# Twelve more row groups take their residual from a DVE transpose that goes through DRAM

## The chip, the cores and the metric

The kernel runs on one core of one Trainium2 chip. The time is microseconds of device time for one execution; lower is better. Engines are named as in the profile: PE (TensorE), DVE (VectorE), ACT (ScalarE), POOL (GpSimd, which also issues DMAs), SP (SyncE, which here only issues DMAs).

## The reference

x is 8 x 3136 x 256. A filter is applied along the sequence by FFT, then a low-rank mix along the sequence, then a two-layer network along the channels, each with its input added back:

```
y = irfft(rfft(x, axis=1) * (filt_r + 1j*filt_i), n=3136, axis=1)
u = y + (y^T @ U @ V)^T            # rank 32, along the sequence
out = u + relu(u @ w_ch1) @ w_ch2  # 256 -> 1024 -> 256
```

The last line matters here: u is used twice, as the input of the first product and as the residual that is added to the second.

## The kernel before, in words

**Two halves.** For each of the 8 batches an FFT half makes u, channels on partitions and sequence along the free dimension, in a tile `ut` (two buffers). The network half then takes u in 49 groups of 512 rows of the flattened 8 x 3136 rows; a group may straddle two batches.

**The FFT half of one batch** is a set of generators that are resumed one piece at a time:

- `later_x` loads x in four chunks (L128, issued by POOL, tile `x`, four buffers).
- `f1` (16 pieces, four for each chunk) does the first DFT on PE (L250), ACT copies it to `asb` (L255), SP writes it to DRAM (`ct1`, `ct0`, L257, L258).
- `mid` (17 pieces) reads it back turned (L331), does the second DFT on PE (L384), multiplies by the filter on DVE (L392, L396, L397: "the products"), does the first inverse DFT on PE (L345) three products later, has ACT copy it (L355), and SP write it to DRAM (`ct2`, L364, three parts).
- `load_e2` has SP read these rows back (L416), into the tile `eb`, in two halves (h = 0 and 1) for each of the three parts: "the rows".
- `rank` makes the low-rank term on PE and ACT (L423 to L435); DVE spreads it over `eb` in four copies (L438).
- `s4` (16 pieces) does the last inverse DFT on PE (L456) from `eb`; DVE (L463) and ACT (L461) copy it into `ut`. The first eight pieces read half 0 of `eb`, the others half 1.

**The network half** has 8 steps for each group, 392 in all. In each step `mm1` makes one of eight slices of the hidden layer of group n (L488), ACT applies the ReLU (L491, one instruction a step, so its n-th instance dates step n), and `mm2` does an eighth of the second product of group n-1 (L544). Every fourth step finishes two 128-row blocks, which DVE moves from PSUM to `och` (L556); every eighth step POOL writes `och` to DRAM (L561, `out`).

**The residual** comes in two ways. For most groups `residual` adds u on PE: `ut` is loaded as weights and multiplied by an identity, eight matmuls of 128 columns for a group that lies in one batch (L536). For a *turned* group (`turned`, number 37 and up, `FIRST_TURNED`) `turn_u` lets DVE transpose u in 32 x 32 blocks (L515, two instructions for a group), SP writes the result to DRAM in four pieces (L520) so that the blocks change place, and reads it back into `tur` (L524); DVE then adds it when it evicts (L552), and PE does nothing.

**The order** is written out by hand. `plan` has a list for each of the 392 steps; after `mm1` and `mm2` of a step, each generator in its list is resumed once. `deal` spreads a generator's pieces over a range of steps. For batch b, a = S[b-1] and z = S[b] are the first steps of batches b-1 and b in the network half (S is 0, 48, 96, 144, 192, 240, 288, 336, and 392 at the end), and e lies 17, 20 or 22 steps before z. Products of batch b run from about a-5 to e-4, rows around e, the low-rank term from e to e+6, `s4` from e+8 to z-2. The plan only sets the order of instructions on each engine. An engine that issues DMAs runs ahead of the steps until something it needs is missing, and what stands behind a waiting instruction on its queue waits too.

Of the kernel before, what the change touches and what calls it, by code (L numbers as in the profile page):

```python
# [10 lines left out]
F16 = mybir.dt.float16  # L11
# [3 lines left out]
NB = 8  # L15
# [3 lines left out]
DM = 256  # L19
# [1 line left out]
NH = 1024  # L21
GT = 512
NG = NB * SEQ // GT
FIRST_TURNED = 37

# [53 lines left out]
def kernel(  # L81
# [11 lines left out]
    nc = tc.nc  # L93
# [15 lines left out]
    sb = ctx.enter_context(tc.tile_pool(name="sb", bufs=1))  # L109
    ps = ctx.enter_context(tc.tile_pool(name="ps", bufs=2, space=bass.MemoryType.PSUM))  # L110

    def bank(tag, name, dtype=F32):

        return ps.tile([128, 512 if dtype == F32 else 1024], dtype, tag=tag, bufs=4 if tag == "z" else 2, name=name)

    def dram(t, off, dims):
        return bass.AP(tensor=t, offset=off, ap=[list(d) for d in dims])
# [5 lines left out]
    xt = {}  # L123

    def load_x(b, c):
        t = sb.tile([98, 8 * DM], F16, tag="x", bufs=4, name="x")
        for a, n in ((0, 96), (96, 2)) if b == 0 else ((0, 98),):
            nc.gpsimd.dma_start(t[a:a + n], dram(x.tensor, (b * SEQ + 8 * c + 32 * a) * DM, [[32 * DM, n], [1, 8 * DM]]))  # L128
        xt[b, c] = t
# [10 lines left out]
    for c in range(4):  # L140
        load_x(0, c)
# [64 lines left out]
    tu = eb[0:RANK, 0:12, :].rearrange("p r d -> p (r d)")  # L206
# [34 lines left out]
    def f1(b):  # L241
        for c in range(4):
            t = xt[b, c].rearrange("p (j d) -> p j d", d=DM)
            asb = sb.tile([98, 8, DM], F16, tag="asb", bufs=4, name="asb")
            for half in range(2):
                for i in range(2):
                    pf = bank("z", "pf")
                    for s in range(2):
                        j = 4 * half + 2 * i + s
                        nc.tensor.matmul(pf[0:98, 256 * s:256 * s + 256],  # L250
                                         ws[:, (8 * c + j) * 98:(8 * c + j + 1) * 98], t[:, j, :],
                                         start=(s == 0), stop=True, skip_group_check=True)
                    dst = asb[:, 4 * half + 2 * i:4 * half + 2 * i + 2, :]
                    src = pf[0:98].rearrange("p (j d) -> p j d", d=DM)
                    nc.scalar.copy(dst, src)  # L255
                    if half and i:
                        nc.sync.dma_start(dram(ct1[b], 8 * c * 96 * DM, [[DM, 96], [96 * DM, 8], [1, DM]]), asb[0:96])  # L257
                        nc.sync.dma_start(dram(ct0[b], 8 * c * DM, [[32 * DM, 2], [1, 8 * DM]]),  # L258
                                          asb[96:98].rearrange("p j d -> p (j d)"))
                    yield  # L260
# [151 lines left out]
    def load_e2(b, part, hs=(0, 1)):  # L412

        n = 12 if (b, part) == (0, 2) else 16
        for h in hs:
            nc.sync.dma_start(eb[32 + part:32 + 4 * n:4, 32 * h:32 * h + 32, :].rearrange("p (q r) d -> p q (r d)", r=8),  # L416
                              dram(ct2[b][part], 8 * h * DM, [[NR * DM, n], [16 * DM, 4], [1, 8 * DM]]))
# [61 lines left out]
    groups = [Group(n) for n in range(NG)]  # L479

    def utv(b):
        return ut[b].rearrange("p h q r -> p h (q r)")
# [11 lines left out]


    def turned(gr):
        return gr.n >= FIRST_TURNED

    def turn_u(gr):

        t = sb.tile([128, 4, 4, 2, 32], F16, tag="asb", bufs=4, name="tu")
        for dh in range(2):
            for b, t0, o, n in gr.seg:
                j, z = o // 32, (o + n) // 32
                while j < z:

                    k = min(z, j + 4 - j % 4) if j % 4 or z - j < 4 else z - z % 4
                    src = utv(b)[:, dh, t0 + 32 * j - o:t0 + 32 * k - o]
                    if k - j < 4:
                        dst = t[:, j % 4:j % 4 + k - j, j // 4, dh, :]  # L510
                        src = src.rearrange("p (c e) -> p c e", e=32)
                    else:
                        dst = t[:, :, j // 4:k // 4, dh, :].rearrange("p c g e -> p g c e")
                        src = src.rearrange("p (g c e) -> p g c e", c=4, e=32)
                    nc.vector.transpose(dst, src)  # L515
                    j = k
            yield
        td = nc.dram_tensor(f"tu_{gr.n}", (128, 4 * DM), F16, kind="Internal")
        for a in range(4):
            nc.sync.dma_start(dram(td, DM * a, [[4 * DM, 32], [128 * DM, 4], [1, DM]]),  # L520
                              t[32 * a:32 * a + 32].rearrange("i c g h e -> i c (g h e)"))
        yield
        gr.tu = sb.tile([128, 4, 4, 2, 32], F16, tag="x", bufs=4, name="tur")
        nc.sync.dma_start(gr.tu.rearrange("p a g h e -> p (a g h e)"), td.ap())  # L524
        yield

    def residual(gr, o, i):
# [10 lines left out]
    def mm2(gr, t):  # L538
        i, half = t // 2, t % 2
        if t % 4 == 0:  # L540
            gr.pc = bank("o", "pc")
        o = gr.pc[:, 256 * (i % 2):256 * (i % 2) + 256]
        for tt in range(4 * half, 4 * half + 4):
            nc.tensor.matmul(o, gr.h[tt][:, 128 * i:128 * i + 128], w2sb[:, tt, :],  # L544
                             start=(tt == 0), stop=(tt == 7 and turned(gr)), skip_group_check=True)
        if half and not turned(gr):
            residual(gr, o, i)
        if t % 4 == 3:
            if t == 3:
                gr.och = sb.tile([128, 4, DM], F32, tag="och", bufs=2, name="och")  # L550
            if turned(gr):
                nc.vector.tensor_add(gr.och[:, i - 1:i + 1, :].rearrange("p g (h a e) -> p (g h) a e", h=2, a=4),  # L552
                                     gr.pc.rearrange("p (f a e) -> p f a e", f=4, a=4),
                                     gr.tu[:, :, i - 1:i + 1].rearrange("p a g h e -> p (g h) a e"))
            else:
                nc.vector.tensor_copy(gr.och[:, i - 1:i + 1, :], gr.pc.rearrange("p (j d) -> p j d", d=DM))  # L556
            if gr.n == NG - 1:
                nc.sync.dma_start(dram(out.tensor, (gr.n * GT + 128 * (i - 1)) * DM, [[DM, 128], [128 * DM, 2], [1, DM]]),
                                  gr.och[:, i - 1:i + 1, :])
            elif t == 7:  # L560
                nc.gpsimd.dma_start(dram(out.tensor, gr.n * GT * DM, [[DM, 128], [128 * DM, 4], [1, DM]]), gr.och)  # L561
# [3 lines left out]
    plan = [[] for _ in range(8 * NG)]  # L565

    def deal(gen, count, a, z):
        for i in range(count):
            plan[max(0, int(a + i * (z - a) / count))].append(gen)

    def later_x(b, c):
        load_x(b, c)
        yield

    f1s = [f1(b) if b > 1 else f1_turned(b) for b in range(NB)]
    mids = [mid(0, "o")] + [mid(b) for b in range(1, NB)]
    ranks = [rank(b) for b in range(NB)]
    s4s = [s4(b) for b in range(NB)]
    turns = [turn_u(gr) for gr in groups]

    u_hat()
# [4 lines left out]
    for i in range(16):  # L586
# [3 lines left out]
        next(f1s[0])  # L590
    nc.gpsimd.dma_start(sv[32:97], sv_d.rearrange("k (r q) -> k r q", q=NQ))
    load_x(1, 0)
    nc.gpsimd.dma_start(w1sb, moe_w_ch1.rearrange("(h dd) c -> dd h c", h=2))
    spread_filters(2)
# [29 lines left out]
    for _ in s4s[0]:  # L624
        pass

    def loads(b, part):
        load_e2(b, part)
        yield

    for b in range(1, NB):
        a, z = S[b - 1], S[b]
        e = z - (17 if b == 1 else 20 if b < 6 else 22)
        deal(mids[b], 13, a + {1: 8, 2: -3}.get(b, -5), e - 4)
        deal(mids[b], 4, e - 4, e)
        for p, at in enumerate((e - 5, e - 4, e + 1)):
            plan[at].append(loads(b, p))
        deal(ranks[b], 6, e, e + 6)
        deal(s4s[b], 16, e + 8, z - 2)
        if b == 1:  # L640
            deal(f1s[1], 12, 1, 8)
        if b + 1 < NB:
            for c in range(4):
                plan[a + (9 + 2 * c if b == 1 else 1 + 4 * c)].append(later_x(b + 1, c))
            deal(f1s[b + 1], 16, a + (21 if b == 1 else 10), z - (13 if b == 1 else 20))

    for gr in groups:
        if turned(gr):
            for i in range(4):
                plan[8 * gr.n + (0, 1, 2, 5)[i]].append(turns[gr.n])  # L650
    for n, gr in enumerate(groups):
        for t in range(8):
            mm1(gr, t)
# [36 lines left out]
```

## Time and profile before

| | us |
|---|---|
| median of 3 runs | 518.17 (514.89 to 519.52) |
| the profiled execution, its own time | 516.43 |
| its span, first to last instruction | 514.6 |
| PE busy | 490.5 (95%) |
| ACT busy | 377.1 (73%) |
| DVE busy | 366.2 (71%) |
| POOL busy | 80.6 (16%) |

The granted TensorE clock is 0.995 of full speed. A share of the span is an average over stages; what a change is worth is read from the stage in which it lies. In a row of a group of instructions, the first number after the bar is the time in which at least one of them ran, the next the mean length of one in ns; matmuls overlap, so the length of one is not what it adds to the time. In a timeline, each line has the start, the length in us, the engine and the line of the code, and in brackets the idle time of the engine before it with what ended that.

### The profile page before, as it was taken

The numbers are of one execution on the slowest core, as the hardware profiler recorded it, in microseconds if no ns is written. First come the engines' busy times: TensorE is split into PE (matmuls) and PEld (weight loads), VectorE is DVE, ScalarE is ACT, GpSimd is POOL, SyncE is SP. The second block draws the span as 40 slices with busy tenths as digits, with TensorE's granted clock in tenths as the row PEclk, the third lists the DMA queues.
The fourth block names the chain that finished last, engine by engine and source line by source line (L and its number), as shares of the span: only waits on it lengthen the run. The fifth ranks groups of instructions, "written<-read, shape, count | busy, mean of one in ns | idle before, by whom it ended". The sixth has DMA issues, their size and how long they took to land.

```text
span 514.6 us, 11909 instructions
## 1 busy us (share of the span) xinstructions
PE 490.5 (95%) x4754; PEld 349.6 (68%) x4754; DVE 366.2 (71%) x497; ACT 377.1 (73%) x704; POOL 80.6 (16%) x122
## 2 busy tenths in 40 slices
PE   3887899999999999999999999999999998999996
PEld 3645566776767777777767777777677765676665
DVE  5886599579847986679747986679846997853332
ACT  6874778867986689667986689667886676666663
POOL 6662010002001110002001110002001000011110
PEclk9998999999999999999999999999999999999999
DMA  8987926957877286837877286837877136644454
GB/s 187 175 206 174 181 74 172 281 171 176 216 229 251 69 186 190 298 130 177 213 227 254 69 185 202 262 156 184 218 228 240 65 126 206 212 153 149 126 162 163
DMA packets 76016, 94.52 MB, mean 184 GB/s; under 512 B 5795, under 2 KB 58979, under 8 KB 75960
## 3 DMA queue, kind: packets, MB, share of 16 engines
q1 hardware_dynamic: 61256, 52.17, 33.9%
q0 software_dynamic: 14704, 41.58, 31.4%
q8 instruction: 37, 0.61, 0.5%
q14 instruction: 19, 0.16, 0.1%
HBM read 58.35 MB, written 50.92 MB: 212 GB/s over the span
## 4 chain that ended last, share of the span: by engine, by line
PE 81%; DVE 8%; DMA 4%; issue 1%; ACT 1%; SPq 0%; POOL 0%; DVEq 0%; POOLq 0%
PE pc L544 31%; PE phh L488 30%; DVE uv L392 5%; PE pu L456 5%; PE pf L250 4%; PE pe L345 4%; PE pz L384 3%; PE pc L536 3%; DMA w2sb<-in_moe_w_ch_dram 2%; PE ph L423 1%; DVE uv L397 1%; DMA eb<-ct 1%; DVE uv L396 1%; DMA ct<-e 1%; DVE och L556 1%
## 5 line engine op out<-in xcount | busy, mean ns | idle before, releaser
L491 ACT ACTIVATE h<-phh 128x512 f16<-128x512 f32 x392 | 235.9, 603 | 83.2 <-PE phh L488 81.7
L544 PE MATMUL pc<-w2sb,h 128*128 128x256 f16 x1568 | 233.7, 272 | 1.2 <-DMA w2sb<-in_moe_w_ch_dram 1.2
L488 PE MATMUL phh<-ut,w1sb 128*128 128x512 f16 (+7 forms) x896 | 233.3, 352 | 0.4 <-DVE ut L463 0.4
L544 PEld LDWEIGHTS <-h 128*128 128x128 f16 x1568 | 151.7, 97 | 91.8 <-issue 1.5
L392 DVE TENSOR_TENSOR uv<-pz,fab 128x1024 f16<-128x1024 f32 (+1 forms) x104 | 120.6, 1177 | 12.5 <-PE pz L384 10.5
L561 POOL DMA_DIRECT2D out_dram<-och x48 | 39.1, 814 | 402.0 <-DVE och L556 318.8
L488 PEld LDWEIGHTS <-w1sb 128*128 128x128 f16 x896 | 78.9, 97 | 19.8 <-issue 1.5
L556 DVE COPY och<-pc 128x512 f32<-128x512 f32 x74 | 51.0, 689 | 44.4 <-PE pc L536 43.5
L355 ACT CAST e<-pe 128x512 f16<-128x512 f32 x96 | 56.6, 591 | 21.0 <-PE pe L345 20.2
L463 DVE CAST ut<-pu 128x392 f16<-128x392 f32 x92 | 48.5, 557 | 17.9 <-PE pu L456 16.0
L255 ACT CAST asb<-pf 98x512 f16<-98x512 f32 x96 | 57.3, 599 | 0.2
L438 DVE COPY eb<-h 32x4096 f16<-32x4096 f16 x32 | 38.2, 1232 | 14.2 <-ACT h L435 14.2
L552 DVE TENSOR_TENSOR och<-pc,tur 128x512 f32<-128x512 f32 x24 | 16.5, 689 | 39.8 <-PE pc L544 37.3
L345 PE MATMUL pe<-uv,m 128*128 128x512 f16 (+1 forms) x117 | 41.3, 371 | 3.6 <-DVE uv L392 1.5
L456 PE MATMUL pu<-sv,eb 97*128 97x49 f16 x1024 | 40.5, 187 | 3.3 <-DMA eb<-ct 3.1
L456 PEld LDWEIGHTS <-eb 97*128 97x128 f16 x1024 | 37.7, 98 | 4.8 <-DVE eb L438 3.4
L536 PE MATMUL pc<-idn,ut 128*128 128x128 f16 (+1 forms) x302 | 40.8, 219 | 0.0
L384 PE MATMUL pz<-a,m 128*128 128x512 f16 x96 | 36.2, 379 | 1.1 <-DVE a L311 1.0
L250 PE MATMUL pf<-x,ws 98*98 98x256 f16 x192 | 36.6, 273 | 0.0
L396 DVE TENSOR_TENSOR uv<-uv 64x1024 f16<-64x1024 f16 (+1 forms) x49 | 30.9, 630 | 1.7
L536 PEld LDWEIGHTS <-ut 128*128 128x128 f16 (+1 forms) x302 | 28.8, 98 | 3.9 <-issue 0.6
L397 DVE TENSOR_TENSOR uv<-uv 64x1024 f16<-64x1024 f16 (+1 forms) x49 | 30.7, 627 | 0.7
(80 smaller groups left out, 264.9 us busy)
## 6 DMA issues: line engine op xcount, KB each, us to landing
out_dram<-och POOLq DMA_DIRECT2D x48, 512.0 KB, 4.4
ct<-e SPq DMA_DIRECT2D x47, 256.0 KB
eb<-ct SPq DMA_DIRECT2D x46, 256.0 KB
x<-in_x_dram POOLq DMA_DIRECT2D x28, 392.0 KB, 7.8
ct<-asb SPq DMA_DIRECT2D x24, 384.0 KB
a<-ct SPq DMA_DIRECT2D x18, 512.0 KB
tu<-tu SPq DMA_DIRECT2D x48, 64.0 KB
tur<-tu SPq DMA_DIRECT2D x12, 256.0 KB
```

Of the source, the lines that this page charges most:

```text
L250: nc.tensor.matmul(pf[0:98, 256 * s:256 * s + 256], ws[:, (8 * c + j) * 98:(8 * c + j + 1) * 98], t[:, j, :], start=(s == 0), stop=True, s ...
L255: nc.scalar.copy(dst, src)
L345: nc.tensor.matmul(pe[:, 0:n], w, uv[:, f, o:o + n], start=(f == 0), stop=(b > 0 or f == 1))
L355: nc.scalar.copy(t[:, 2 * (i % 2):2 * (i % 2) + 2, :].rearrange("p k d -> p (k d)"), pe)
L384: nc.tensor.matmul(pz, a2m, src[:, k:k + 2, :].rearrange("p k d -> p (k d)"), start=True, stop=True)
L392: nc.vector.tensor_mul(uv[:, :, o:o + n], zin, fin)
L456: nc.tensor.matmul(pu[:, NQ * i:NQ * i + NQ], eb[:, 8 * n + i, d], sv[:, 8 * g + i, :], start=(i == 0), stop=True, skip_group_check=True)
L488: nc.tensor.matmul(ph[:, o:o + n], w1sb[:, dh, 128 * t:128 * t + 128], utv(b)[:, dh, t0:t0 + n], start=(dh == 0), stop=(dh == 1), skip_gro ...
L491: nc.scalar.activation(h, ph, RELU)
L536: nc.tensor.matmul(d, w, idn, start=False, stop=(dh == 1), skip_group_check=True)
L544: nc.tensor.matmul(o, gr.h[tt][:, 128 * i:128 * i + 128], w2sb[:, tt, :], start=(tt == 0), stop=(tt == 7 and turned(gr)), skip_group_check ...
L556: nc.vector.tensor_copy(gr.och[:, i - 1:i + 1, :], gr.pc.rearrange("p (j d) -> p j d", d=DM))
```

## The change

For batches 1 to 6 (b in the loop over the plan), the last two groups before the border step z, numbers z/8-2 and z/8-1, are turned as well: 4, 5, 10, 11, 16, 17, 22, 23, 28, 29, 34 and 35. `turn_at` holds the four steps at which each group's generator is resumed. For the first of the two the DVE transposes are at e-3 and e-2, for the second at e-1 and e; the writes to DRAM are at z-14 and z-13, the reads at z-10 and z-8. These DMAs are issued by POOL; those of the old turned groups stay with SP. `FIRST_TURNED` becomes 38, so group 37 has its residual on PE again. So 23 groups are turned instead of 12.

The new tiles have tags of their own, `tu` and `tur`, two buffers each; `x` and `asb` have three buffers instead of four, and three of the first x chunks use buffers of `asb`. The fourth x chunk of a batch is loaded two steps later (a+15, not a+13), for batch 2 ten steps later (25, not 15).

The rows of batches 1 to 7 are read half by half: half 0 of the three parts where both halves were (e-5, e-4, e+1), half 1 of all three at e+2.

```
-FIRST_TURNED = 37
+FIRST_TURNED = 38
     def load_x(b, c):
-        t = sb.tile([98, 8 * DM], F16, tag="x", bufs=4, name="x")
+        tag = "asb" if (b, c) in ((0, 3), (1, 0), (1, 1)) else "x"
+        t = sb.tile([98, 8 * DM], F16, tag=tag, bufs=3, name="x")
...
     def turned(gr):
-        return gr.n >= FIRST_TURNED
+        return gr.n >= FIRST_TURNED or gr.n in turn_at
     def turn_u(gr):
-        t = sb.tile([128, 4, 4, 2, 32], F16, tag="asb", bufs=4, name="tu")
+        t = sb.tile([128, 4, 4, 2, 32], F16, tag="tu", bufs=2, name="tu")
...
+        queue = nc.sync if gr.n >= FIRST_TURNED else nc.gpsimd
         for a in range(4):
-            nc.sync.dma_start(dram(td, DM * a, [[4 * DM, 32], [128 * DM, 4], [1, DM]]),
+            queue.dma_start(dram(td, DM * a, [[4 * DM, 32], [128 * DM, 4], [1, DM]]),
...
-        gr.tu = sb.tile([128, 4, 4, 2, 32], F16, tag="x", bufs=4, name="tur")
-        nc.sync.dma_start(gr.tu.rearrange("p a g h e -> p (a g h e)"), td.ap())
+        gr.tu = sb.tile([128, 4, 4, 2, 32], F16, tag="tur", bufs=2, name="tur")
+        queue.dma_start(gr.tu.rearrange("p a g h e -> p (a g h e)"), td.ap())
...
-    def loads(b, part):
-        load_e2(b, part)
+    def loads(b, parts, h):
+        for part in parts:
+            load_e2(b, part, [h])
         yield
+    turn_at = {n: [8 * n + i for i in (0, 1, 2, 5)] for n in range(FIRST_TURNED, NG)}
...
-        for p, at in enumerate((e - 5, e - 4, e + 1)):
-            plan[at].append(loads(b, p))
+        for at, parts, h in ((e - 5, [0], 0), (e - 4, [1], 0), (e + 1, [2], 0), (e + 2, range(3), 1)):
+            plan[at].append(loads(b, parts, h))
+        if b < NB - 1:
+            turn_at[z // 8 - 2] = [e - 3, e - 2, z - 14, z - 10]
+            turn_at[z // 8 - 1] = [e - 1, e, z - 13, z - 8]
...
-                plan[a + (9 + 2 * c if b == 1 else 1 + 4 * c)].append(later_x(b + 1, c))
+                plan[a + (9 + 2 * c + 10 * (c > 2) if b == 1 else 1 + 4 * c + 2 * (c > 2))].append(later_x(b + 1, c))
...
-    for gr in groups:
-        if turned(gr):
-            for i in range(4):
-                plan[8 * gr.n + (0, 1, 2, 5)[i]].append(turns[gr.n])
+    for n, at in turn_at.items():
+        for i in at:
+            plan[i].append(turns[n])
```

## The prediction, made before the changed kernel was run

> **What bounds the kernel now.** I read the page first, then the waits of PE, then the timeline of single steps, and last DVE's timeline where it feeds PE.
>
> ```profile
> PE 490.5 (95%) x4754; PEld 349.6 (68%) x4754; DVE 366.2 (71%) x497; ACT 377.1 (73%) x704; POOL 80.6 (16%) x122
> ...
> L536 PE MATMUL pc<-idn,ut 128*128 128x128 f16 (+1 forms) x302 | 40.8, 219 | 0.0
> ```
>
> PE is busy nearly all the time, and the residual (L536) has 302 matmuls in it. Whether PE sets the time everywhere is told by its waits, asked for 62 to 430 us, which is the network half with batches 1 to 7 beside it:
>
> ```profile
> PE pz L384 <- DVE a L311: 1.0, 2, 0.7
> ```
>
> This is the whole answer: 1.0 us in 368. So between 62 and 430 us every PE instruction lengthens the run by what it takes on PE. What a residual matmul takes is read from PE's timeline of bare steps:
>
> ```profile
> 152.32 0.59 PE L488 MATMUL phh<-ut,w1sb 128*128 128x512 f16 x2
> 152.75 0.60 PE L544 MATMUL pc<-w2sb,h 128*128 128x256 f16 x4
> 153.19 0.59 PE L488 MATMUL phh<-ut,w1sb 128*128 128x512 f16 x2
> 153.62 0.60 PE L544 MATMUL pc<-w2sb,h 128*128 128x256 f16 x4
> 154.06 0.28 PE L536 MATMUL pc<-idn,ut 128*128 128x128 f16 x2
> 154.17 0.59 PE L488 MATMUL phh<-ut,w1sb 128*128 128x512 f16 x2
> ```
>
> From L488 to L488 is 0.87 us without residual and 0.98 with two of its matmuls: 0.055 us each. By the page's row it would be 40.8/302 = 0.135, but that row counts overlapped time, so I take 0.055.
>
> After 430 us PE waits once for the products of batch 7:
>
> ```profile
> 432.12 0.39 PE L345 MATMUL pe<-uv,m 128*128 128x512 f16 x1 [1.33 <-DVE uv L397]
> ```
>
> Before it DVE runs without a gap from 401.1 us, and the chain that ended last goes through DVE from 410.6 to 432.1, with group 37's transposes in it:
>
> ```profile
> 416.50 0.71 DVE tu L515
> 417.21 1.11 DVE uv L392
> 418.32 0.62 DVE tu L515
> ```
>
> **Part 1, the residual of twelve groups leaves PE.** Each lies in one batch: 8 matmuls x 0.055 = 0.44 us, twelve times 5.28 us. Group 37 gives 0.44 back, so 88 matmuls net, 4.84 us. By 0.135 it would be 11.9 us, the upper bound of this term.
>
> **Part 2, group 37's transposes leave DVE.** In DVE's timeline they displace 0.64 and 0.61 us (start to next start), 1.25 together, in a stretch that ends in PE's wait. This has to be summed with part 1, since DVE and not PE sets the time there. DVE becomes saturated around step 284 (399.6 us). By then PE is ahead by the ten groups of batches 1 to 5 (4.4 us) and half of group 34 (0.2). From there DVE's string ends 1.25 us earlier: 4.6 + 1.25 = 5.9 us ahead when it releases PE. PE by itself would be 5.28 - 0.44 + 1.33 = 6.2 ahead, so it still waits some 0.3 us and **5.9 us** is the gain at 432 us. Behind that the plan is the old one, so 5.9 reaches the end. Turned evictions cost the same: L552 and L556 both take 689 ns.
>
> **Part 3, the new transposes on DVE.** Four for each of six batches, 0.69 us each (L515, 688 ns): 2.75 us a batch. They stand where DVE has nothing to do, between the last product and the low-rank copies:
>
> ```profile
> 260.32 0.69 DVE L556 COPY och<-pc 128x512 f32<-128x512 f32 x1
> 265.39 0.69 DVE L556 COPY och<-pc 128x512 f32<-128x512 f32 x1 [4.38 <-PE pc L536]
> 268.72 1.22 DVE L438 COPY eb<-h 32x4096 f16<-32x4096 f16 x1 [2.64 <-ACT h L435]
> ```
>
> Two fill 1.4 of the 4.38 us, two 1.4 of the 2.64. In batch 6 the gap is 5.33 us, in batch 1 3.67 and 1.91. I cost them at nothing; without that cover it would be 6 x 2.75 = 16.5 us of DVE time, most of it late for the low-rank copies and so for `s4`.
>
> **Part 4, the trip through DRAM on POOL's queue.** This is what the trace does not show: these DMAs from SP are there, from POOL not. Take the batch whose border is z = 192. On POOL's queue stand `out` (issued at 271.15), eight writes, the first read, the next `out`, the second read. An issue took POOL 0.54 to 0.57 us for an x chunk and 0.75 to 0.80 for `out`, so the writes are out by about 277. The `out` ahead of them landed at 277.64; four writes of 64 KB behind it should land by 279.3. Then the read is issued; a DMA from POOL of twice its size (`out`) lands at best after 3.1 us, so I put it at 282.3. It is needed by the eviction at z-5, which DVE began at 283.76: 1.5 us in hand. The same for the other borders, with `out` landing at 163.22, 219.51, 336.53, 396.24: +0.5, +2, +0.6 and -0.5 us in hand. Border 48 has its writes at step 34 and its need at 43, some 10 us.
>
> If it is late by L, DVE stands still by L, with the last `ut` copies and the products of the next batch behind it. What that costs PE is told by the room between DVE's end of a product and PE's L345 that takes it. The first product of each batch has least: 1.26 us at batch 5, 0.92 to 1.27 elsewhere. PE now comes 0.5 us sooner, so some 0.7 us of lateness is free, and beyond that PE loses L - 0.7 in each batch. Best case L below 0.7 everywhere, no cost. Worst by the rows: a POOL transfer's longest landing is 9.0 us, against the 3.1 that I used, so L = 4 to 5 and some 6 x 4 = 24 us. My estimates lie near the low end; I take 0.3 us in all.
>
> **Where the Trainium skill speaks against this.** One `out` in each batch stands beside the low-rank copies of DVE and is longer:
>
> ```profile
> 155.36 1.13 POOL L561 DMA_DIRECT2D out_dram<-och  x1 [9.07 <-DVE och L556]
> ```
>
> 1.13 us, against 0.75 to 0.80 elsewhere. The Trainium skill, "SBUF — State Buffer", section "Who interferes with whom", says that GpSimd and a VectorE copy in a two-port mode exclude each other for whole instructions, so that descriptors of a GpSimd DMA wait for it. The trace agrees for the issue, 0.35 us longer. By that rule the writes could not begin before the low-rank copies end, and the sum would be about 0.5 us higher at z = 96, where they end at 158.6.
>
> **Part 5, three x buffers, and the fourth chunk later.** The chunk now stands behind the `out` of step a+15 on POOL's queue, where it stood in front. An x chunk just behind an `out` lands 6.0 to 6.3 us after its issue. Issued 0.8 us after that `out`, it lands at 142.0, 199.6, 259.1, 315.4 and 373.7 us for batches 3 to 7, and PE takes it (L250) at 144.2, 201.9, 260.0, 317.7 and 376.2: 0.9 to 2.5 us in hand. For batch 2 it is 93.5 against 95.1, but there the `out` itself landed only at 93.05, and x cannot be before it. Best case nothing. Worst by the rows: the second chunk in a row lands after 8 to 9 us, which would cost 0 to 1.5 us a batch, 3 us in all. I take 0.3 us, for batch 2.
>
> **Part 6, rows by halves.** PE does not wait for rows in 62 to 430 us, so nothing is gained; half 1 is issued at e+2 (about 271 us at z = 192) and needed at 280.9, so nothing is lost. SP's queue has four row reads in a row where it had two, so the reads of the next batch's DFT (L331) start 1.2 us later, at 273 instead of 271.8; they are needed from 283.3.
>
> **Sum:** 5.9 - 0.3 - 0.3 = 5.3 us. The profiled execution took 516.43 (span 514.6), so 511.1 by it. The median of the runs is 1.7 us higher, which would give 512.9. Three runs that spread over 4.6 us do not tell which is typical; I take the middle, **512.0 us**.
>
> **Rivals.**
>
> *The read from DRAM is late and stalls DVE at z-5.* For it: four of five borders have less than 2 us in hand, and DMA is 0.8 to 0.9 busy there. Against: after 282 us DMA is idle until 291. Its place is the eviction at z-5, its price 6 x (L - 0.7): it eats the whole gain at L = 1.7 us and makes the kernel slower by 1% from L = 2.5. With L = 3, 6 x 2.3 = 13.8, so about 520 to 522 us. Chance 0.16.
>
> *The fourth x chunk is late and PE waits at L250.* For it: the 0.9 us at batch 5. Against: that `out` no longer shares the DMA engines with the chunk that stood in front. Worst 3 us: 514.5. With part of both rivals the gain is 1 to 5 us. Chance 0.30.
>
> *DVE takes over as the bound once PE is faster.* PE gains 0.9 us from z-8 to z+8, just where DVE is 98% busy (286 to 294 us). Against: the smallest room is 1.24. If that were all used in each batch, half of part 1 would go, 2.6 us: 514.6. Chance 0.08.
>
> *The forecast* as it stands, 509.5 to 513.5, has 0.46.
>
> **Chances.** Faster by over 1% (a gain of over 5.2 us) 0.42: most of the forecast's case. Within 1% 0.42: its rest and the second and third rivals. Slower by over 1% 0.16. About 1% is what this kernel's runs can tell from no change. The range is 508.0, for a gain that misses the costs and runs as low as the lowest ones shown, to 519.0, which takes in the x chunks, a DVE bound and an L of up to 2.
>
> **What the profile after would show.** L536 with 214 matmuls; steps at z-8 to z-1 of 0.87 us, where nothing else stands in them; L515 without idle time behind it at e; no wait of PE on DVE at batch borders; the wait at 432 us down to about 0.3. Wrong if L552 waits for DMA `tur` by more than 0.7 us at z-5, if L252 on PE (the old L250) waits for DMA x, or if POOL's second `out` after e is held up far enough to keep `och` from DVE.

## The result, and the profile after

The changed kernel takes 521.8 us (median of 6 runs, 521.27 to 528.0); in the same comparison the kernel before takes 515.04. The ratio is **1.0137, 95% interval 1.010 to 1.0174**: slower by 1.4%, where 1% faster was forecast. The profiled execution took 521.29 us (span 519.5), against 516.43 (514.6) before. The ratios here and below leave out runs over 1.5% slower than the fastest of the same kernel, but for the one kernel where the text gives all four times.

The page of the changed kernel, and from its groups by line the residual on PE:

```profile
PE 488.0 (94%) x4666; PEld 343.9 (66%) x4666; DVE 378.0 (73%) x519; ACT 376.7 (73%) x704; POOL 121.5 (23%) x182
```

```profile
L540 PE MATMUL pc<-idn,ut 128*128 128x128 f16 (+1 forms) x214 | 28.7, 220 | 0.0
```

The 88 matmuls are gone (302 before, 214 now). But the span grew while PE's busy time fell. PE's waits in 62 to 445 us say where (columns: who waits at which line for whom, us in total, times, longest). Before, the same list had 1.3 us for batch 7 (L345), the 1.0 us at L384 and 0.2 us at L456:

```profile
PE pu L458 <- DVE ut L465: 4.2, 3, 1.7
PE pz L386 <- DVE uv L394: 3.1, 4, 0.8
PE pz L386 <- DVE a L313: 1.0, 2, 0.7
PE pe L347 <- DVE uv L399: 0.8, 1, 0.8
PE pf L252 <- DMA x<-in_x_dram: 0.3, 1, 0.3
```

PE now waits for DVE in `s4` (L458) and at the first products of the next batch (L386). DVE's timeline at the border z = 192 shows what DVE itself waits for:

```profile
288.08 0.69 DVE L556 TENSOR_TENSOR och<-pc,tur 128x512 f32<-128x512 f32 x1 [3.53 <-DMA tur<-tu]
288.68 0.55 DVE L465 CAST ut<-pu 128x392 f16<-128x392 f32 x1
289.16 1.21 DVE L394 TENSOR_TENSOR uv<-pz,fab 128x1024 f16<-128x1024 f32 x1
```

The first eviction of the first turned group stands 3.53 us for its read from DRAM, with the last `ut` copies and the first product queued behind it. Before, the eviction at this place had 0.62 us of idle time ahead of it, waiting for PE:

```profile
283.76 0.69 DVE L556 COPY och<-pc 128x512 f32<-128x512 f32 x1 [0.62 <-PE pc L536]
```

The first ReLU of each group of eight steps, dated in both traces, gives the loss by border. From eight steps before a border to eight steps after it, the difference after minus before moves by +0.2, +3.5, +3.6, +1.1 and -0.6 us at z = 96, 144, 192, 240 and 288, and PE should have gained 0.88 in each (16 matmuls). So the cost is 1.1, 4.4, 4.4, 1.9 and 0.3 us, **12.1 us in all** against a gain of 5.3. Batch 7 gains another 0.5 us (steps 304 to 323). By step 16 the changed kernel is already 1.6 us ahead; the traces of the twelve kernels with the new plan, which is the same up to there, lie between 2.0 us ahead and 0.6 behind at this step, so this is not put down to the change. Together that makes 4.7 us more, and the span has 4.9. At z = 48 there is no cost: the difference falls by 0.83 us from step 40 to 56, as the matmuls that are gone would have it.

POOL's timeline at z = 192 shows the trip link by link:

```profile
272.68 1.13 POOL L565 DMA_DIRECT2D out_dram<-och  x1 [9.06 <-DVE och L560]
273.80 5.00 POOL L524 DMA_DIRECT2D tu<-tu  x7
281.70 0.55 POOL L524 DMA_DIRECT2D tu<-tu  x1 [2.91 <-DMA out_dram<-och]
284.95 0.56 POOL L528 DMA_DIRECT2D tur<-tu  x1 [2.70 <-DMA tu<-tu]
285.50 0.76 POOL L565 DMA_DIRECT2D out_dram<-och  x1
286.55 0.55 POOL L528 DMA_DIRECT2D tur<-tu  x1 [0.29 <-issue]
```

`out` landed at 281.42, 8.7 us after its issue. The eighth write was not issued before that; the fourth write landed at 284.37, and only then could the read go, which landed at 287.95. The transposes had been finished since 263.9 and 268.8 us:

```profile
262.56 1.30 DVE L517 STREAM_TRANSPOSE tu<-ut 128x512 f16<-128x512 f16 x2
266.91 0.69 DVE L560 COPY och<-pc 128x512 f32<-128x512 f32 x1 [3.04 <-PE pc L540]
267.52 1.29 DVE L517 STREAM_TRANSPOSE tu<-ut 128x512 f16<-128x512 f16 x2
270.25 1.22 DVE L440 COPY eb<-h 32x4096 f16<-32x4096 f16 x1 [1.43 <-ACT h L437]
```

They fill idle time of DVE, as forecast (4.38 became 3.04, and 2.64 became 1.43). Their result lay ready for 5 to 10 us before POOL, waiting to issue `out`, came to it.

### The profile page after: what moved, and what is told of

Read it like the earlier page. It is cut to its first block, busy times and chain, and to the rows that moved or that the text cites. A ratio compares the mean times of both kernels' runs of the same rounds, so it can differ in the third digit from the quotient of the medians.

```text
span 519.5 us, 11773 instructions
## 1 busy us (share of the span) xinstructions
PE 488.0 (94%) x4666; PEld 343.9 (66%) x4666; DVE 378.0 (73%) x519; ACT 376.7 (73%) x704; POOL 121.5 (23%) x182
## 4 chain that ended last, share of the span: by engine, by line
PE 59%; DMA 14%; DVE 10%; issue 7%; POOL 4%; ACT 1%; SPq 0%; DVEq 0%; POOLq 0%
PE pc L548 23%; PE phh L490 22%; DMA tu<-tu 7%; DVE uv L394 5%; PE pf L252 4%; DMA tur<-tu 3%; PE pe L347 3%; DMA x<-in_x_dram 3%; PE pz L386 3%; POOL tu L524 2%; PE pu L458 2%; PE pc L540 1%; POOL out_dram L565 1%; DVE och L556 1%; DVE och L560 1%
## 5 line engine op out<-in xcount | busy, mean ns | idle before, releaser
L556 DVE TENSOR_TENSOR och<-pc,tur 128x512 f32<-128x512 f32 x46 | 31.7, 690 | 55.4 <-PE pc L548 38.6
L560 DVE COPY och<-pc 128x512 f32<-128x512 f32 x52 | 35.7, 687 | 28.8 <-PE pc L540 28.1
L458 PE MATMUL pu<-sv,eb 97*128 97x49 f16 x1024 | 39.2, 185 | 6.8 <-DVE ut L465 4.2
L347 PE MATMUL pe<-uv,m 128*128 128x512 f16 (+1 forms) x117 | 41.3, 371 | 3.1 <-DVE uv L394 1.6
L458 PEld LDWEIGHTS <-eb 97*128 97x128 f16 x1024 | 37.3, 96 | 9.2 <-issue 7.2
L386 PE MATMUL pz<-a,m 128*128 128x512 f16 x96 | 36.7, 384 | 4.2 <-DVE uv L394 3.1
L524 POOL DMA_DIRECT2D tu<-tu x48 | 33.9, 714 | 10.6 <-DMA out_dram<-och 10.6
L517 DVE STREAM_TRANSPOSE tu<-ut 128x512 f16<-128x512 f16 (+2 forms) x50 | 30.2, 643 | 0.2
## 6 DMA issues: line engine op xcount, KB each, us to landing
out_dram<-och POOLq DMA_DIRECT2D x48, 512.0 KB, 3.8
a<-ct SPq DMA_DIRECT2D x18, 512.0 KB
```

Source lines behind the costliest of these rows:

```text
L347: nc.tensor.matmul(pe[:, 0:n], w, uv[:, f, o:o + n], start=(f == 0), stop=(b > 0 or f == 1))
L386: nc.tensor.matmul(pz, a2m, src[:, k:k + 2, :].rearrange("p k d -> p (k d)"), start=True, stop=True)
L458: nc.tensor.matmul(pu[:, NQ * i:NQ * i + NQ], eb[:, 8 * n + i, d], sv[:, 8 * g + i, :], start=(i == 0), stop=True, skip_group_check=True)
L524: queue.dma_start(dram(td, DM * a, [[4 * DM, 32], [128 * DM, 4], [1, DM]]), t[32 * a:32 * a + 32].rearrange("i c g h e -> i c (g h e)"))
```

## The experiments

Each ratio is against the kernel before, on the same chip.

**One group in place of two.** Two theories were set against each other. Theory A: the first read lands after its eviction wants it. Theory B: the trips load POOL and the DMA engines and cost wherever they stand.

```
-            turn_at[z // 8 - 2] = [e - 3, e - 2, z - 14, z - 10]
             turn_at[z // 8 - 1] = [e - 1, e, z - 13, z - 8]
```

> Only the second of the two groups before each border is turned (5, 11, 17, 23, 29, 35); the first has its residual on PE again, everything else is as in the changed kernel. Theory A (the first read from DRAM lands after the eviction at z-5 wants it, and DVE, then PE, stand still): the second read is wanted eight steps later, so DVE does not wait for tur, and the kernel is faster than before by 6 x 0.44 of PE and most of group 37's 1.25 us of DVE, 2.5 to 3.5 us. Rival B (the trips load POOL and the DMA engines, and that costs wherever they stand): half of the loss stays, 3 us slower than before.

512.87 against 516.24 us: 0.9934 (0.9908 to 0.996), 3.4 us faster. DVE does not wait for `tur` in 62 to 445 us, and the idle time ahead of the eviction at z-5 is 0.62 us again. As theory A has it.

**No group before a border.**

```
-        if b < NB - 1:
-            turn_at[z // 8 - 2] = [e - 3, e - 2, z - 14, z - 10]
-            turn_at[z // 8 - 1] = [e - 1, e, z - 13, z - 8]
```

> No group before a border is turned; group 37 has its residual on PE, x and asb have three buffers, the fourth x chunk is later and the rows are read by halves, as in the changed kernel. Theory A: about 1.2 us faster than before (group 37's transposes leave DVE's string), since none of these parts costs anything. Rival C (the fourth x chunk or the rows by halves carry the loss): 2 us or more slower than before, with PE waiting for x at L252 or for rows at L458.

514.36 against 516.24: 0.9971 (0.9945 to 0.9996), 1.5 us faster. Between 62 and 445 us PE waits only for the 1.0 us at L386 (two waits) that it had before at L384. The buffers, the late chunk and the rows by halves carry none of the loss.

**Reads that wait for nothing.** The same number of bytes, the same transposes and writes; but the reads no longer wait for the writes, and go out ahead of them (at z = 192 some 10 us).

```
+        if gr.n < FIRST_TURNED:
+            gr.tu = sb.tile([128, 4, 4, 2, 32], F16, tag="tur", bufs=2, name="tur")
+            nc.gpsimd.dma_start(gr.tu.rearrange("p a g h e -> p (a g h e)"), dram(ct2[0][0], 0, [[4 * DM, 128], [1, 4 * DM]]))
         t = sb.tile([128, 4, 4, 2, 32], F16, tag="tu", bufs=2, name="tu")
...
+        if gr.n < FIRST_TURNED:
+            return
         gr.tu = sb.tile([128, 4, 4, 2, 32], F16, tag="tur", bufs=2, name="tur")
```

> As the changed kernel, but the 12 reads of POOL take as many bytes of rows that have lain in DRAM since batch 0, and stand ahead of the transposes in the order, so that they wait for nothing; the transposes and the 48 writes are as they were. The residual of these 12 groups is therefore not theirs. Theory A: no wait for tur, so the gain that was forecast appears, 5 to 6 us against before. Rival B: the writes and POOL's work are all there, so it stays slower than before by 3 us or more.

511.11 against 516.24: 0.9893 (0.9865 to 0.9922), **5.5 us faster**. So the transposes, the writes and POOL's extra issues cost next to nothing, and the forecast gain is there once the read is in time. Theory B falls.

**The trip on SP's queue.**

```
-        queue = nc.sync if gr.n >= FIRST_TURNED else nc.gpsimd
+        queue = nc.sync
```

> As the changed kernel, but SP issues the writes and reads of the 12 groups, behind the rows and ahead of the reads of the next batch's DFT. Theory A with POOL's queue as what makes the read late (the out of step z-17 ahead of the writes): the read is in tur before z-5, DVE does not wait, and the DFT's reads, some 6 us later than before, cost PE 0 to 2 us a batch: between 5 us faster and 3 us slower than before. If the load of the DMA engines made it late, whoever issues: DVE waits at z-5 for 2 us or more as in the changed kernel.

523.67 against 516.24: 1.014 (1.0111 to 1.0169). `tur` is in time at z = 96 to 288 (0.51 us idle ahead of the eviction, 1.38 at 288), at z = 48 it is 3.1 us late. The cost has moved, as SP's timeline at z = 192 and PE's waits show:

```profile
277.09 6.36 SPq L524 DMA_DIRECT2D tu<-tu  x8
283.62 1.55 SPq L528 DMA_DIRECT2D tur<-tu  x2
285.22 0.43 SPq L333 DMA_DIRECT2D a<-ct  x1
```

```profile
PE pz L386 <- DMA a<-ct: 8.1, 6, 2.7
```

Eight writes and the two reads that wait for them stand ahead of the DFT's reads, 1.6 MB a batch, which now go out after 285 and not at 277, when the writes begin; PE waits for them at L386. Its trace also has three stretches of 3.41 us with a granted clock of 0.50 (from 114.0, 230.1 and 349.6 us; see the last section). The trip was early enough, what stood behind it was not. The direction was left open by theory A; the 0 to 2 us a batch for the DFT's reads was too low.

**What makes POOL's trip late.** Three suspects were taken away: DVE's low-rank copies, which run while POOL issues `out` and the first writes; the DFT's reads, which share the DMA engines; the rows' second halves, which the change put just ahead. A fourth run takes the first two away together, a fifth halves the writes. The first, thinner low-rank copies:

```
+            m = 16 if b in (0, 7) else 1
-            nc.vector.tensor_copy(eb[0:32, 16 * g:16 * g + 16, :],
+            nc.vector.tensor_copy(eb[0:32, 16 * g:16 * g + m, :],
...
```

> As the changed kernel, but in batches 1 to 6 the four low-rank copies of DVE (L440) write one sixteenth of their columns, so that DVE is free while POOL issues the out of step z-17 and the writes. The low-rank term of these batches is therefore missing in most of u. Theory D (the copies hold up POOL's descriptors): out at the borders 144 to 288 lands 4 to 5 us after its issue in place of 5.2 to 9.2, the first read 3 us or more sooner, DVE waits for tur under 1 us a batch, and the kernel is 3 to 6 us faster than before. Theory E (the reads of the next batch's DFT on SP's queue take the DMA engines): the landings and the wait stay, 4 us or more slower than before.

Fewer reads for the DFT:

```
+            if g in (1, 2) and b < 7:
+                a2[g] = a2[0]
+                return
```

> As the changed kernel, but in batches 2 to 6 two of the three 512 KB reads for the DFT (L333) are left out and the first tile is used three times, so that 1 MB less is read just when POOL's out and writes are under way. Two thirds of the frequencies of these batches are therefore wrong. Theory E: out and the writes land 3 us or more sooner, DVE waits for tur under 1 us a batch at the borders 96 to 240 (batch 7 is unchanged), 2 to 6 us faster than before. Theory D: the first packets still come only when the copies end, out lands about 2 us sooner at most, the read is late by 1 us or more, and the kernel is not faster than before by more than 2 us.

Both edits together:

> Thin low-rank copies and fewer DFT reads together (the low-rank term and two thirds of the frequencies of batches 1 or 2 to 6 are therefore not right). If the two together make POOL's transfers late: out at the borders 96 to 240 lands 4 to 5 us after its issue, the idle time ahead of the first eviction at these borders is the 0.6 us of before, and the kernel is 4 us or more faster than before. If the order on POOL's queue makes it (out, eight writes, the read): the idle time stays over 1 us at two or more of these four borders and the gain is under 3 us.

Only the first of the two groups, with half the writes:

```
-            turn_at[z // 8 - 1] = [e - 1, e, z - 13, z - 8]
```

> Only the first of the two groups before each border is turned (4, 10, 16, 22, 28, 34), with its DMAs where the changed kernel has them: four writes between out and the read in place of eight. If the number of writes makes the read late: the read lands 1 to 2 us sooner, DVE waits under 2 us for it, and the time is within 2 us of before. If it is the out ahead of them and the traffic of SP: DVE waits about 3 us at borders 144 and 192 as in the changed kernel, TensorE's clock falls to half behind it, and it is 4 us or more slower than before.

The rows read whole, as before the change:

```
-        for at, parts, h in ((e - 5, [0], 0), (e - 4, [1], 0), (e + 1, [2], 0), (e + 2, range(3), 1)):
-            plan[at].append(loads(b, parts, h))
+        for p, at in enumerate((e - 5, e - 4, e + 1)):
+            plan[at].append(loads(b, p))
...
```

> As the changed kernel, but the rows are read as before, both halves of a part at once, so that 512 KB of them no longer stand just ahead of out and the writes. If these rows make the trip late: out and the writes land 1 to 2 us sooner at borders 144 to 288, the idle time ahead of the first eviction falls from 2.5 to 3.5 to under 2 us, the half clock is gone, and the kernel is within 2 us of before. If they don't: it stays 4 us or more slower than before.

Measured, with the idle time of DVE ahead of the first eviction (0.51 to 0.62 when nothing is late, 1.4 to 1.5 at z = 288):

| | ratio (95%) | z = 96 | 144 | 192 | 240 | 288 |
|---|---|---|---|---|---|---|
| changed kernel | 1.0137 (1.010 to 1.0174) | 1.8 | 3.5 | 3.5 | 2.7 | 2.5 |
| thin copies | 1.0002 (0.9967 to 1.0036) | 1.4 | 1.4 | 1.5 | 2.8 | 2.5 |
| fewer DFT reads | 0.9961 (0.9923 to 0.9999) | 0.9 | 1.6 | 0.5 | 1.6 | 3.2 |
| both | 0.9941 (0.9908 to 0.9974) | 0.6 | 0.9 | 4.8 | 1.6 | 2.8 |
| first group only | 1.0263 (1.020 to 1.0326) | 1.6 | 5.6 | 2.7 | 2.0 | 3.2 |
| rows whole | 1.0126 (1.0068 to 1.0185) | 2.3 | 3.2 | 3.0 | 2.5 | 2.9 |

Each row of idle times is one execution; the one of "both" was the slowest of its ten (516.72 us, the others 509.7 to 515.4), so its borders need not be typical. The ratio of the first group only counts all four runs, 524.3, 525.4, 533.0 and 533.9 us; the two lower ones alone are 1.7% slower than before.

Neither theory holds alone. Without the copies, POOL's timeline at z = 192 has

```profile
270.26 0.78 POOL L566 DMA_DIRECT2D out_dram<-och  x1 [9.05 <-DVE eb L441]
271.03 3.83 POOL L525 DMA_DIRECT2D tu<-tu  x7
277.95 0.55 POOL L525 DMA_DIRECT2D tu<-tu  x1 [3.09 <-DMA out_dram<-och]
280.63 0.57 POOL L529 DMA_DIRECT2D tur<-tu  x1 [2.12 <-DMA tu<-tu]
```

The issues are shorter (0.78 in place of 1.13, seven writes in 3.83 in place of 5.00), as the rule of the Trainium skill ("SBUF — State Buffer", "Who interferes with whom") has it. But `out` still takes 7.4 us to land (270.26 to 277.67), and at the four borders 144 to 288 it lands after 6.7 to 9.3 us, where 4 to 5 were expected. With fewer DFT reads it still takes 7 to 9 us there, though the last writes land closer behind it. With both gone the first two borders are within 0.4 us of being in time, and one read at z = 192 took 5.7 us to land (278.44 to 284.17) with no reason that the trace shows. Half the writes do not help either: at z = 144 the read was issued 2.2 us after the fourth write had landed, and DVE stood 5.6 us. The rows' halves play no part. So copies and traffic each add a microsecond or two at some of the borders, and how much each of them adds, and what makes `out` land late without either, **stays open**. What is common to all six rows is that the trip begins behind `out`.

**Writes ahead of `out`.** The two parts that write and read are put right behind the two that transpose.

```
-            turn_at[z // 8 - 2] = [e - 3, e - 2, z - 14, z - 10]
-            turn_at[z // 8 - 1] = [e - 1, e, z - 13, z - 8]
+            turn_at[z // 8 - 2] = [e - 3, e - 2, e - 1, e + 2]
+            turn_at[z // 8 - 1] = [e - 1, e, e + 1, e + 4]
```

> As the changed kernel, but the writes of the two groups stand at e-1 and e+1, ahead of the out of step z-17 on POOL's queue, and the reads at e+2 and e+4. Theory A: the first read has landed before z-5, DVE does not wait for tur; the rows, whose transfers are now beside the writes, may be up to 2 us later and have some 2 us of room before L458: 3 to 6 us faster than before. If the rows have no room: PE waits at L458 for eb, up to 2 us a batch, and it is from 0 to 6 us slower than before.

511.97 against 516.05: 0.9917 (0.9892 to 0.9943), 4.3 us faster. DVE is back to 0.51 us ahead of the eviction (1.38 at z = 288). PE waits at L458 three times, 1.2 us at z = 48, 0.6 at 144 and 0.5 at 288.

**The same from border 96 on.** With the first border as in the changed kernel:

```
-            turn_at[z // 8 - 2] = [e - 3, e - 2, e - 1, e + 2]
-            turn_at[z // 8 - 1] = [e - 1, e, e + 1, e + 4]
+            turn_at[z // 8 - 2] = [e - 3, e - 2] + ([z - 14, z - 10] if b == 1 else [e - 1, e + 2])
+            turn_at[z // 8 - 1] = [e - 1, e] + ([z - 13, z - 8] if b == 1 else [e + 1, e + 4])
```

> As the run with the writes ahead of out, but at the first border (48) writes and reads stand where the changed kernel has them, since the run before waited 1.4 us there at L458 and the changed kernel did not. Theory A: DVE waits nowhere for tur, PE loses at most 0.7 us at two borders: 4.5 to 6 us faster than before, 1 to 1.5 us faster than with the writes ahead everywhere. If the 1.4 us were chance: no faster than that run, 3 to 4 us faster than before.

510.24 against 515.92: **0.9904 (0.9878 to 0.9929), 5.0 us faster** than before; this version beats both kernels. Over the run above, a gain of 1 to 1.5 us had been expected; it is 0.7 us by the centres of the two ratios, and their intervals overlap, so it is not shown. PE waits at L458 for 0.2 us at z = 96 and 0.8 at 288. Its POOL timeline at z = 192, and the first eviction:

```profile
257.08 0.79 POOL L565 DMA_DIRECT2D out_dram<-och  x1 [9.42 <-DVE och L560]
258.42 2.21 POOL L524 DMA_DIRECT2D tu<-tu  x4 [0.54 <-DVE tu L517]
263.35 3.02 POOL L524 DMA_DIRECT2D tu<-tu  x4 [2.73 <-DVE tu L517]
266.37 1.51 POOL L528 DMA_DIRECT2D tur<-tu  x1
267.87 1.34 POOL L565 DMA_DIRECT2D out_dram<-och  x1
```

```profile
279.31 0.69 DVE L556 TENSOR_TENSOR och<-pc,tur 128x512 f32<-128x512 f32 x1 [0.51 <-PE pc L548]
```

The writes now wait for nothing but the transposes; the read is issued 12.9 us before its eviction and lands at 273.1, 6.7 us after its issue, where the sum of part 4 had 3.1, and still 6 us early.

## Why the prediction was wrong

**The step that failed is part 4**, in both of its figures.

*The landing.* Part 4 put the first read of z = 192 11.1 us after the issue of `out` (271.15 to 282.3). It was 15.3 (272.68 to 287.95). By link: `out` itself 8.7 in place of 6.5, the four writes 3.0 behind it in place of 1.7, the read's issue 0.6 behind them and its landing 3.0 behind that. The read was sized well, its issue was put at nothing; `out` was taken from the trace of before, where nothing stood behind it, and the writes from a guess. I had taken the lowest row for the links that were not shown and kept the longest one (9.0 us) only for an end of the range that the range then did not reach. I had +0.5, +2, +1.5, +0.6 and -0.5 us in hand. Counted from the 0.51 us (1.38 at z = 288) of the runs with a read in time, the measured lateness was 1.3, 3.0, 3.0, 2.2 and 1.1 us.

*Its price.* "Some 0.7 us of lateness is free, and beyond that PE loses L - 0.7" was read from the room between a product and L347. But PE does not get that far. At z = 144, 192 and 240 it stops at L458, two steps on, because DVE's `ut` copies stand behind the waiting eviction; the rest comes at L386, which is where z = 96 has its only wait. PE's timeline at z = 144, changed kernel:

```profile
225.47 0.60 PE L548 MATMUL pc<-w2sb,h 128*128 128x256 f16 x4
227.72 0.37 PE L458 MATMUL pu<-sv,eb 97*128 97x49 f16 x8 [1.65 <-DVE ut L465]
228.84 0.38 PE L386 MATMUL pz<-a,m 128*128 128x512 f16 x1 [0.76 <-DVE uv L394]
229.06 0.59 PE L490 MATMUL phh<-ut,w1sb 128*128 128x512 f16 x2
229.49 0.93 PE L548 MATMUL pc<-w2sb,h 128*128 128x256 f16 x4
```

The costs 1.1, 4.4, 4.4, 1.9 and 0.3 us stand against latenesses 1.3, 3.0, 3.0, 2.2 and 1.1: nearly all of L at z = 96 and 240, 1.4 us more than L at z = 144 and 192, and 0.8 less at 288. I named the `ut` copies as queued behind the eviction and then did not ask who waits for them. By L - 0.7 the measured latenesses would have cost 7.1 us, so the landing, which part 4 priced at 0.3 us, is the larger error. Of the 5.0 us above that, some 3.4 are a halved clock behind the two longest stalls (see the last section), and only the rest is room that was not there.

The rival had the right mechanism and place, and a price too low: its L = 3 at six borders was to cost 13.8 us; a mean of 2.1 at five cost 12.1. Its time does not follow from its own sum: 512.0 less the 0.3 us already in it, plus 13.8, is 525.5 and not 520 to 522. That the measured 521.8 lies in that stretch is luck.

**What was right.** Part 1: 0.055 us a matmul; the reads that wait for nothing gained 5.5 us, where 5.9 less some waits had been forecast, and z = 48 gained 0.83 of 0.88. Part 2: group 37 off DVE with the other parts is 1.5 us (0.2 to 2.8), forecast 1.25; in the trace of the run without border groups, steps 304 to 323 gain 1.24. In the changed kernel PE's wait for batch 7 is down from 1.33 to

```profile
437.60 0.39 PE L347 MATMUL pe<-uv,m 128*128 128x512 f16 x1 [0.76 <-DVE uv L399]
```

where 0.3 had been forecast; in the run whose reads wait for nothing, where PE is as early as forecast, it is 0.2. Part 3: no cost. Part 5: PE waits 0.3 us for x, at one place, as taken. Part 6: neither gain nor loss, and with the rows whole it is as slow. The low-rank copies do lengthen POOL's issues, by what the Trainium skill ("SBUF — State Buffer", "Who interferes with whom") says; but without them the time only falls to that of before, 1.4% or 7 us, where half a microsecond at one border had been reckoned for them. Part 4 took that row as a remark and not into its sum.

## What to carry to other kernels

A tile that goes out and comes back through DRAM is a chain of DMAs, each of which waits for the one before; size each link by the slow rows of the busiest stretch, and issue the first as soon as the data is there. On an engine that only issues DMAs, look for what stands ahead on its queue: here an `out` that waited for an eviction held back writes whose data had been ready for up to 10 us. Price a late operand by the first thing that stops behind the waiting instruction, of any kind, not by the consumer that one has in mind.

## What was not expected of the hardware

**A stall of PE costs more than its length.** The windows of the changed kernel behind the stall at z = 144 (columns: stretch, busy us of PE, PEld, DVE, ACT and POOL with instructions, granted clock, DMA share, GB/s):

```profile
226.00:229.60 3.60, 1.19 (x14) 0.66 (x12) 3.10 (x5) 0.81 (x2) 0.00 (x0) 1.00 0.30 86
229.60:233.00 3.40, 3.40 (x16) 2.02 (x14) 3.32 (x6) 1.19 (x2) 0.00 (x0) 0.50 0.03 5
233.00:236.00 3.00, 3.00 (x27) 2.43 (x26) 2.29 (x3) 2.13 (x4) 1.87 (x3) 1.00 0.43 175
```

After 3.6 us with PE busy for 1.19, the granted clock is 0.50 for 3.41 us, and then full again: four matmuls of a step take 0.85 us from start to next start and not 0.43. That is 1.7 us on top of the stall, and accounts for the two borders that cost 4.4 us; at the three others, with stalls of 2 us and less, the clock stayed at 1.00. The Trainium skill, "TensorE: Matmul & The Clock Gate", section "Part 1: The HAM clock gate (the "warmup" mystery)", has the half clock and its window of about 3.4 us, and puts it behind an idle window. The trace agrees with the size and length; here it came although PE had worked for a third of the time before. In the trace of before there is no such stretch between the first step (51 us) and 512.8 us, only one just ahead of it at 45.2 to 48.6 us, and it stood in no part of the prediction.

How much idle time it takes can be read from the traces. The stretches lie on a grid: 229.61 and 291.05 us, where two of them begin, are 18 windows of 3.413 us apart. From 60 to 445 us, in the traces of before and of all twelve kernels with the new plan, PE was busy for 11 to 51% of the window ahead in the ten cases where a half clock followed, and for 52% or more in all other windows. The changed kernel has 33% at z = 144, 29% at 192 and 57% at 240. As far as these traces go, PE's busy share of such a window decides, with an edge near half, and not one long gap: the longest at z = 144 is 1.65 us.

**A ninth DMA of POOL waits for the first.** In the changed kernel and in the run with thin copies, the eighth write is issued only when the `out` eight DMAs ahead of it has landed (281.42 and 281.70; 277.67 and 277.95). Whether that is the chip's limit or that of the program's semaphores the runs do not tell.
